# An FNet and GEGLU kernel on one core: width transform ahead of the sequence transform, both by seven products

## The chip, the core and the metric

The kernel runs on one core of one Trainium2 chip, in one launch. TensorE (PE in the profile) multiplies matrices into PSUM, VectorE (DVE) and ScalarE (ACT) do elementwise work, GpSimd (POOL) and SyncE (SP) here issue DMAs. Each engine works through a queue of its own; semaphores tie the queues together. The metric is the device time of a run in microseconds. Before the change the median of three runs is 816.8 us (816.44 to 816.83).

## What is computed

The input x has 2048 rows of 512. Its layer norm xn goes two ways, and both results are added to x:

```python
a = einsum("bsd,ed->bse", x, dft_hid_re)      # x is xn here
b = einsum("bsd,ed->bse", x, dft_hid_im)
y = einsum("ts,bse->bte", dft_seq_re, a) - einsum("ts,bse->bte", dft_seq_im, b)
...
h = gelu(einsum("bsd,df->bsf", x, w_gate)) * einsum("bsd,df->bsf", x, w_up)
return einsum("bsf,fd->bsd", h, w_down)
```

The first three lines are the Fourier branch: a width transform (512 by 512, real and imaginary) and a sequence transform (2048 by 2048, real and imaginary). The last two are the GEGLU branch with 1792 hidden columns. Everything is float32.

## The kernel before

A float32 product is made of three matmuls: each operand is split into a high part (`split_hi`, on ACT, a copy to fp32r, line 68) and a low part (`split_lo`, on DVE, source minus high part, line 73), and `mm3` (line 84) adds high by high, high by low and low by high into one PSUM bank. Every matmul of weight has a 128 by 128 stationary and a 128 by 512 moving operand.

Most products of two matrices cut in 2 by 2 blocks are done with seven block products in place of eight, which needs sums of blocks beforehand on DVE and sums of results afterwards.

The instructions of each engine run in the order in which the program issues them (`tc.manual_schedule()`); what is prepared ahead is written out by hand. The stages in order:

- Normalisation of the 16 panels of x (`ln_begin`, `ln_end`, `ln_split`), mixed with the sequence transform of the first 512 output rows (`seq`, z). That is done plainly: 16 panels, two matrices, four column blocks, three matmuls, 384 in all.
- `y_part` multiplies the result of a chunk of 512 rows by the width matrices (96 matmuls per chunk), `y_store` adds x and stores to HBM (`partial`).
- The three other chunks (`steps`, 24 per two passes): `load_step`, `sum_step` and `split_step` prepare the matrix panels two to four steps ahead, `products` makes 3 or 4 of the seven products of a step, 1008 matmuls in all. Behind each chunk `y_part` follows.
- x is normalised a second time, transposed, in between (`early_xT`).
- 28 units of GEGLU (`unit`), 14 for each half of the rows. A unit makes seven products of 6 matmuls (`product`); `background` lists the work on DVE and ACT that prepares the next units and `run` spreads it over the unit; `fill` puts products of the down projection (`down`, 6 matmuls each) between. Their sums go to `partial` in HBM by accumulating DMAs on POOL.
- `finish` and `last_down` make the output from the seven sums and `partial`.

All SBUF tiles come from one pool of 109 slots of 2 KB per partition. PSUM has 8 banks.

Of the kernel before, what the change touches and what calls it, by code (L numbers as in the profile page):

```python
# [8 lines left out]
F32 = mybir.dt.float32  # L9
# [5 lines left out]
P = 128  # L15
# [8 lines left out]
TPC = CH // P  # L24
SPT = 2 * TPC
HD = D // 2
HS = NS // 2
WARM = 11
SLOTS = 109
# [5 lines left out]
def fnet_geglu_kernel(ctx: ExitStack, tc: tile.TileContext, x, xt, cs, dh, wgu, wd, out):  # L35
# [4 lines left out]

    nc = tc.nc

    const = ctx.enter_context(tc.tile_pool(name="const", bufs=1))
    mem = ctx.enter_context(tc.tile_pool(name="mem", bufs=SLOTS))
# [7 lines left out]

    def ps_tile(name):
        return psum.tile([P, D], F32, name=name, tag="ps")

    def hl_tile(name):

        return slot(name + "h", F32R), slot(name + "l", F32R)  # L60

    def hl_half(name):

        t = slot(name, F32R, (P, 2, HD))
        return t[:, 0], t[:, 1]

    def split_hi(t, src, sign=1):
        nc.scalar.activation(t[0], src, AF.Copy, scale=float(sign))  # L68

    def split_lo(t, src, sign=1, engine=nc.vector):  # L70
        hi = t[0].bitcast(F32)
        if sign > 0:
            engine.tensor_sub(t[1], src, hi)  # L73
        else:
            engine.scalar_tensor_tensor(t[1], src, -1.0, hi, op0=OP.mult, op1=OP.subtract)

    def split(t, src, sign=1, engine=nc.vector):
        split_hi(t, src, sign)
        split_lo(t, src, sign, engine)

    def mm3(ps, a, sl, b, first, last, resumed=False, part=slice(3), late=0):

        for r, (u, v) in list(enumerate(((0, 0), (late, 1 - late), (1 - late, late))))[part]:
            nc.tensor.matmul(ps, a[u][:, sl], b[v], start=first and r == 0, stop=last and r == 2,  # L84
                             skip_group_check=resumed)
# [4 lines left out]
    stats = const.tile([P, 2, NS], F32, name="stats")  # L90
    ident = const.tile([P, P], F32, name="ident")
    eps = const.tile([P, 1], F32, name="eps")
    mean_rstd = dram.tile([2, NS, P], F32, name="mean_rstd")

    partial = dram.tile([NC // 2, 7, 2, P, CH], F32, name="partial")
    xT_hl = dram.tile([7, 2, 2, P, CH], F32, name="xT_hl")
    xnt = dram.tile([NC // 2, 2, ND, P, CH], F32, name="xnt")


    xs, ln, xn = {}, {}, {}  # L100

    def load_x(n):
        if n < NS:
            xs[n] = slot(f"x{n}")
            if n:
                nc.sync.dma_start(xs[n], x[n])
            else:
                for h, queue in enumerate((nc.sync, nc.scalar)):
                    queue.dma_start(xs[n][:, h * HD:(h + 1) * HD], x[n, :, h * HD:(h + 1) * HD])

    def ln_begin(n):
        parts = 1 if n else 2
        bn = small.tile([P, parts, 6], F32, name="bn")
        for h in range(parts):
            nc.vector.bn_stats(bn[:, h], xs[n][:, h * HD:(h + 1) * HD] if parts > 1 else xs[n])
        nc.vector.bn_aggr(stats[:, :, n], bn)
        ln[n] = small.tile([P, 2], F32, name="w")
        nc.scalar.activation(ln[n][:, 0:1], stats[:, 1, n:n + 1], AF.Abs_reciprocal_sqrt, bias=eps)
        nc.scalar.activation(xs[n], xs[n], AF.Identity, bias=stats[:, 0, n:n + 1], scale=-1.0)

    def ln_end(n):
        r, t = (ln[n][:, i:i + 1] for i in range(2))
        var = stats[:, 1, n:n + 1]

        nc.vector.scalar_tensor_tensor(t, var, EPS, r, op0=OP.add, op1=OP.mult)
        nc.vector.scalar_tensor_tensor(t, t, 0.5, r, op0=OP.mult, op1=OP.mult)
        nc.vector.scalar_tensor_tensor(var, t, 1.5, r, op0=OP.subtract, op1=OP.mult)
        xn[n] = hl_half(f"xa{n}"), hl_half(f"xb{n}")
        for h in range(2):
            nc.scalar.activation(xn[n][h][0], xs[n][:, h * HD:(h + 1) * HD], AF.Copy, scale=var)  # L130
        nc.scalar.activation(xs[n], xs[n], AF.Copy, scale=var)

    def ln_split(n):
        ln.pop(n)
        for h in range(2):
            split_lo(xn[n][h], xs[n][:, h * HD:(h + 1) * HD])


    seq = [(n, m) for n in range(NS - 2) for m in range(2)]
    seq += [(n, m) for m in range(2) for n in (NS - 2, NS - 1)]  # L140
    raws, panels, dhl = {}, {}, {}

    def load_panel(i):
        if i < len(seq):
            n, m = seq[i]
            raws[i] = slot("pan")
            nc.sync.dma_start(raws[i], cs[0, m, n])

    def split_panel(i, part=slice(2)):
        if i < len(seq):  # L150
            if part.start is None:
                panels[i] = hl_tile("pan")
                split_hi(panels[i], raws[i])
            if part.stop is None or part.stop == 2:
                split_lo(panels[i], raws.pop(i))

    draw = {}

    def load_d(i):
        if 0 <= i < 2 * ND:  # L160
            draw[i] = slot("d")
            nc.sync.dma_start(draw[i], dh[i // ND, i % ND])

    def split_d(i, part):
        if 0 <= i < 2 * ND:
            if part == 0:
                dhl[divmod(i, ND)] = hl_tile(f"d{i}")
# [46 lines left out]

    yps, yx = {}, {}

    def load_y(c):
        for j in range(TPC):
            yx[j] = slot("yx")
            nc.sync.dma_start(yx[j], xt[c // 2, c % 2, j])  # L220

    Y_ORDER = [(1, 0), (1, 1), (0, 2), (0, 3), (1, 2), (1, 3), (0, 0), (0, 1)]
    Y_FIRST = [(m, d) for m in range(2) for d in range(ND)]

    def y_part(q, js=range(TPC), order=Y_ORDER):

        for j in js:
            if q == 0:
                yps[j] = ps_tile("y")
            for part in (slice(2), slice(2, 3)):  # L230
                for r in range(2):
                    m, d = order[2 * q + r]
                    mm3(yps[j], dhl[m, d], cols(j), z[m, d], q == r == 0, q == 3 and r == 1, part=part, late=1)

    def y_store(c, js=range(ND)):

        sp, t = divmod(c, 2)
        for j in js:
            nc.vector.tensor_add(yx[j], yps[j], yx[j])
        for j in js:  # L240
            if t and j < 2:
                nc.vector.tensor_sub(yx[j], yx[j], yx[j + 2])
            nc.sync.dma_start(partial[sp, (1, 3, 2, 4)[2 * t + j // 2], j % 2], yx[j])

    def store_stats():
        ps = ps_tile("st")
        nc.tensor.transpose(ps[:2 * NS, :P], stats.rearrange("p a b -> p (a b)"), ident)
        t = slot("st")
        nc.vector.tensor_copy(t[:2 * NS, :P], ps[:2 * NS, :P])
        nc.sync.dma_start(mean_rstd.rearrange("a b c -> (a b) c"), t[:2 * NS, :P])  # L250

    PANELS = {0: ((0, 0), (1, 0), (1, 1)), 1: ((0, 0), (1, 0), (0, 1), (1, 1))}
# [726 lines left out]
```

## Time and profile before

| | us |
|---|---|
| median of three runs | 816.8 |
| span of the profiled execution | 815.6 |
| PE busy | 810.1 |
| DVE busy | 703.6 |
| ACT busy | 478.7 |
| POOL busy | 97.1 |

The profile shows one execution. Busy times are the union of an engine's instructions, so two that overlap count once. "Releaser" is the instruction whose end let another start. A timeline row has the start in us from the span's start, the duration in us, engine, line, operation, outputs and inputs, shapes and count. A window row has the width of a stretch, busy times of PE, PEld (weight loads), DVE, ACT and POOL with the number of instructions in brackets, the granted clock, the share of the DMA engines that was busy, and GB/s.

### The profile page before, as it was taken

How to read it: one execution, taken by the hardware profiler on the slowest of the kernel's cores; microseconds unless marked ns; L12 is line 12 of the kernel's file. 1: busy time of each engine (PE TensorE's matmuls, PEld its weight loads, DVE VectorE, ACT ScalarE, POOL GpSimd, SP SyncE). 2: the span in 40 equal slices, each digit the busy share in tenths (PEclk: the TensorE clock that was granted, in tenths of full speed). 3: DMA queues.
4: the chain of work that ended last, by engine and by line, in shares of the span. 5: the costliest groups of instructions: out<-in, count | busy, mean ns of one | idle time of the engine just before them, and what ended most of it. 6: DMA issues, size and time to landing. Idle time of an engine off the chain costs nothing. (4 is left out here: it accounts for less than half of the span.)

```text
span 815.6 us, 11284 instructions
## 1 busy us (share of the span) xinstructions
PE 810.1 (99%) x3558; PEld 665.5 (82%) x3558; DVE 703.6 (86%) x1300; ACT 478.7 (59%) x910; POOL 97.1 (12%) x132
## 2 busy tenths in 40 slices
PE   9999999999999999999999999999999999999998
PEld 6888888888888888888788888888888888888886
DVE  6677998998899997999779998888787778989787
ACT  6787535543255343644366768767666777675564
POOL 0000000000100000000001412422221233222100
PEclk9999999999999999999999999999999999999999
DMA  9900438664796838763332967768976787787942
GB/s 329 378 16 1 168 130 282 196 191 150 245 371 205 276 123 302 257 227 104 119 115 80 259 138 155 171 138 200 262 127 123 129 220 157 165 209 138 246 106 104
DMA packets 79084, 149.15 MB, mean 183 GB/s; under 512 B 9104, under 2 KB 9648, under 8 KB 79024
## 3 DMA queue, kind: packets, MB, share of 16 engines
q1 hardware_dynamic: 63408, 115.13, 42.5%
q0 software_dynamic: 15328, 33.04, 21.9%
q8 instruction: 28, 0.46, 0.2%
q14 instruction: 32, 0.26, 0.1%
q10 hardware_dynamic: 288, 0.26, 0.1%
HBM read 106.95 MB, written 41.44 MB: 182 GB/s over the span
## 5 line engine op out<-in xcount | busy, mean ns | idle before, releaser
L68 ACT ACTIVATE psh<-pan 128x512 fp32r<-128x512 f32 x168 | 97.0, 626 | 107.8 <-DVE pan L281 32.2
L73 DVE TENSOR_TENSOR psl<-pan,psh 128x512 fp32r<-128x512 f32 x168 | 105.5, 685 | 3.7 <-ACT psh L68 3.5
L543 POOL DMA_DIRECT2D partial<-part x82 | 71.9, 894 | 222.6 <-ACT part L539 201.9
L84 PE MATMUL m<-psl,xch 128*128 128x512 f32 x192 | 74.9, 390 | 0.3 <-DVE psl L73 0.3
L84 PE MATMUL m<-psh,xch 128*128 128x512 f32 x192 | 74.8, 390 | 0.0
L84 PE MATMUL m<-psh,xcl 128*128 128x512 f32 x192 | 74.7, 389 | 0.0
L539 ACT ACTIVATE part<-dn 128x512 f32<-128x512 f32 x94 | 55.4, 605 | 24.2 <-PE dn L84 22.4
L73 DVE TENSOR_TENSOR wl<-ws,wh 128x512 fp32r<-128x512 f32 x84 | 55.0, 684 | 0.1
L68 ACT ACTIVATE wh<-ws 128x512 fp32r<-128x512 f32 x84 | 49.4, 629 | 0.0
L766 DVE TENSOR_TENSOR w<-c,w 128x512 f32<-128x512 f32 x28 | 19.3, 690 | 31.8 <-ACT w L763 31.8
L763 ACT ACTIVATE w<-b 128x512 f32<-128x512 f32 x28 | 16.8, 598 | 49.1 <-PE b L84 49.1
L84 PE MATMUL z<-panh,xa 128*128 128x512 f32 x128 | 44.7, 390 | 0.0
L84 PE MATMUL z<-panh,xb 128*128 128x512 f32 x128 | 44.6, 389 | 0.0
L393 POOL DMA_DIRECT2D xnt<-xr x16 | 8.9, 555 | 297.9 <-DVE xr L382 297.9
L84 PEld LDWEIGHTS m<-psl,xch 128*128 128x128 f32 x192 | 36.0, 188 | 8.4 <-DVE psl L73 1.0
L84 PEld LDWEIGHTS m<-psh,xch 128*128 128x128 f32 x192 | 36.0, 188 | 7.6
L84 PEld LDWEIGHTS m<-psh,xcl 128*128 128x128 f32 x192 | 36.0, 188 | 7.4
L73 DVE TENSOR_TENSOR htl<-s,hth 128x512 fp32r<-128x512 f32 x56 | 36.0, 686 | 5.2 <-ACT hth L68 5.2
L512 DVE TENSOR_TENSOR s<-s 128x512 f32<-128x512 f32 x56 | 37.5, 688 | 1.0
L73 DVE TENSOR_TENSOR wl<-wx,wh 128x512 fp32r<-128x512 f32 x28 | 19.2, 687 | 19.3 <-ACT wh L68 19.3
L68 ACT ACTIVATE hth<-s 128x512 fp32r<-128x512 f32 x56 | 32.4, 643 | 2.0 <-DVE s L512 2.0
L84 PE MATMUL m<-psh,xa 128*128 128x512 f32 x96 | 33.5, 389 | 0.0
(393 smaller groups left out, 2357.7 us busy)
## 6 DMA issues: line engine op xcount, KB each, us to landing
pan<-in_cs SPq DMA_DIRECT2D x200, 256.0 KB, 4.4
partial<-part POOLq DMA_DIRECT2D x94, 256.0 KB, 4.7
wx<-in_wgu SPq DMA_DIRECT2D x56, 256.0 KB, 4.6
wd<-in_wd SPq DMA_DIRECT2D x28, 256.0 KB, 4.3
acc<-partial SPq DMA_DIRECT2D x28, 256.0 KB, 5.2
yx<-in_xt SPq DMA_DIRECT2D x16, 256.0 KB, 4.4
partial<-yx SPq DMA_DIRECT2D x16, 256.0 KB, 2.3
xr<-in_xt SPq DMA_DIRECT2D x16, 256.0 KB, 5.1
```

What stands on the lines that cost most here:

```text
L68: nc.scalar.activation(t[0], src, AF.Copy, scale=float(sign))
L73: engine.tensor_sub(t[1], src, hi)
L84: nc.tensor.matmul(ps, a[u][:, sl], b[v], start=first and r == 0, stop=last and r == 2, skip_group_check=resumed)
L393: nc.gpsimd.dma_start(xnt[sp, t, d], xr[sp, d, t])
L512: nc.vector.tensor_sub(t, u, v)
L539: nc.scalar.activation(t, ps[j], AF.Copy)
L543: nc.gpsimd.dma_start(partial[sp, r, j], t, accum_op=OP.add)
L763: nc.scalar.activation(w, b, AF.Copy)
L766: nc.vector.tensor_add(w, c, w)
```

## The change

The width transform comes first. `spectral(sp, k, i)` makes product k of seven for panel i of a half (`sp`) of the rows: 6 matmuls, with the transposed x as stationary and the width matrices (`w1`) as moving operand. The first half's transposed x is made on PE from the normalised panels (`transpose_x`); its seven block operands xT stay for the first 14 units. The results a and b go to HBM (`ab`). The matrices w1 (seven pairs of high and low tiles) and the second half's xT are parked in HBM (`park`, on POOL) and fetched again (`fetch`, on SP) around unit 13; behind unit 13 stands spectral of the second half, then units 14 to 27.

The sequence transform comes last, as 4 passes of 16 steps (`steps`), for both halves of the output. It goes on in PSUM banks that are seeded from the down projection's sums in `partial`: three products per step in the first two passes, four in the last two. Its panels come from HBM as before; a and b are loaded and split beside the first pass (`early_side`) and the second (`late_side`). `drain` makes the output. x itself enters through DMAs from `xt` to `partial` in HBM and through `load_residual`. SBUF is now 43 slots of 4 KB per partition and 23 of 2 KB.

The core of the diff (the old stages named above go; unit keeps its seven products):

```diff
-WARM = 11
-SLOTS = 109
+WARM = 12
+BIG = 43
+SLOTS = 23
...
+    def first_half(n):
+        b11, b21 = halves(pts[n])
+        split_hi(xT_part(0, n), b11)
+        split_hi(xT_part(1, n), b21)
+        xq[n] = slot("xq")
+        nc.scalar.activation(xq[n], pts[n], AF.Copy)
+        split_lo(xT_part(0, n), b11)
+        split_lo(xT_part(1, n), b21)
...
+    def spectral(sp, k, i):
...
+        for j in range(2):
+            mm3(ps[i], [v[:, j] for v in xT[k]], cols(i), [v[:, j] for v in w1[k]], k in (0, 4) and j == 0, j == 1,
+                resumed=k not in (0, 4))
+        if k == 0:
...
+            nc.scalar.activation(sb[i], sa[i], AF.Copy)
...
+        elif k == 6:
+            s6[i] = slot("s6")
+            nc.scalar.activation(s6[i], sb[i], AF.Copy)
+        elif k == 3:
+            t = slot("b")
+            nc.scalar.activation(t, sb[i], AF.Copy, scale=-1.0)
+            to_ab(n, 1, t)
+        elif k == 4:
+            neg_sub(s6[i], sa[i], s6[i])
+            to_ab(n + TPC, 1, s6[i])
...
+    for n in range(TPC, SPT):
+        transpose_x(n)
+        second_half(n)
+        if n + 1 < SPT:
+            ln_apply(n + 1)
+        split(xT_part(5, n - TPC), xsum[n - TPC][5])
+        spectral(0, 5, n - TPC)
...
+    def side_work(k, f, src):
+        for j in range(2):
+            if f:
+                f(j)
+            w1_part(k, src, slice(j, j + 1))
+        for i in range(TPC):
+            split(xT_part(k, i), xsum[i][k])
...
+    side_work(*more[0])
+    for k, (f, *rest) in zip((6, 3, 4), more[1:]):
+        for i in range(TPC):
+            spectral(0, k, i)
+        side_work(f, *rest)
+    add_w(0)
+    split_w(0)
...
         def multiply(k, ps, first=False):
             product(n, k, ps, first)
-            if (n, k) in FETCH:
-                fetch_xT(FETCH[n, k])
+            if n == NP - 1:
+                xT[k] = fetch(xT_hl, k, "xT")
+                if k == 0:
+                    w1[0] = fetch(w1_hl, 0, "w1")
...
+    for p, k in enumerate(S_ORDER):
+        for i in range(TPC):
+            spectral(1, k, i)
+            if i == 0:
+                while carry:
+                    carry.pop(0)()
+                if p + 1 < len(S_ORDER):
+                    w1[S_ORDER[p + 1]] = fetch(w1_hl, S_ORDER[p + 1], "w1")
+    for n in range(NP, 2 * NP):
+        unit(n)
...
+    while carry:
+        carry.pop(0)()
+    for i in range(SUM_AHEAD):
+        sum_step(i)
+    for k in range(4):
+        h_sum(NP - 1, k)
+    for i in range(SPLIT_AHEAD):
+        split_step(i)
+    for n in range(SIDE_AHEAD):
+        early_side(n)
...
+    def contract(i, r, j):
+        c, g, n = steps[i]
+        mm3(bank[c, r, j], side(r, n), cols(j), pan_hl[i, r], False, n == NS - 1, resumed=True)
```

`S_ORDER` is (0, 1, 5, 6, 3, 4, 2). The head before the loop over panels 4 to 7 prepares panels 0 to 3 one by one: `ln_stats`, `ln_first`, `ln_apply`, `transpose_x`, `first_half`, `w1_part`, with `spectral(0, 0, i)` and `spectral(0, 1, i)` between, and then `w1_sums` with `w1_part(5)` and the statistics of panels 4 to 7. `background` of units 0 and 1 takes the statistics of the second half's panels, units 4 and 5 normalise its transposed rows (`norm_xr`), and units 6 to 11 split and park them. The last four `spectral(0, 2, i)` are items between the products of units 0 and 1.

More of the change, by code (lines that the diff above doesn't have):

```diff
@@ L65, in hl_half, with split_hi, split_lo, split @@
         return t[:, 0], t[:, 1]
[L67 to L83, printed above, removed]
+    def split_hi(t, src):
+        nc.scalar.activation(t[0], src, AF.Copy)
+    def split_lo(t, src):
+        nc.vector.tensor_sub(t[1], src, t[0].bitcast(F32))
+    def split(t, src):
+        split_hi(t, src)
+        split_lo(t, src)
+    def neg_sub(dst, u, v):
+        nc.vector.scalar_tensor_tensor(dst, u, -1.0, v, op0=OP.mult, op1=OP.subtract)
+    def mm3(ps, a, sl, b, first, last, resumed=False, late=0):
+        for r, (u, v) in enumerate(((0, 0), (late, 1 - late), (1 - late, late))):
             nc.tensor.matmul(ps, a[u][:, sl], b[v], start=first and r == 0, stop=last and r == 2,
@@ L133, in ln_split @@
[L133 to L155, printed above, removed]
@@ L225, in y_part, with ln_scale @@
[L225 to L243, printed above, removed]
+    def ln_scale(n0, n1, rstd):
+        var = stats[:, 1, n0:n1]
+        w = small.tile([P, 2, n1 - n0], F32, name="w")
+        r, t = w[:, 0], w[:, 1]
+        nc.scalar.activation(r, var, AF.Abs_reciprocal_sqrt, bias=eps)
+        nc.vector.scalar_tensor_tensor(t, var, EPS, r, op0=OP.add, op1=OP.mult)
+        nc.vector.scalar_tensor_tensor(t, t, -0.5, r, op0=OP.mult, op1=OP.mult)
+        nc.vector.scalar_tensor_tensor(rstd, t, 1.5, r, op0=OP.add, op1=OP.mult)
@@ new lines, in w1_part, with transpose_x, halves @@
+    def w1_part(k, src, j=slice(2), part=slice(2)):
+        if k not in w1:
+            w1[k] = [pair(f"w1{k}{h}") for h in "hl"]
+        t = [v[:, j] for v in w1[k]]
+        for f in (split_hi, split_lo)[part]:
+            f(t, src[:, j])
+    def transpose_x(n):
+        pts[n] = ps_tile("pt")
+        for j in range(ND):
+            nc.tensor.transpose(pts[n][:, cols(j)], xs[n][:, cols(j)], ident)
+    def halves(t):
+        v = t.rearrange("p (h j t) -> p h j t", h=2, j=2)
+        return v[:, 0], v[:, 1]
@@ L518, in h_split @@
         return hl[q, r], hs[q, H_PLACE[(1, 3, 0, 2)[k]]]
[L520 to L524 removed]
+    D_ORDER = (0, 2, 1, 5, 4, 6, 3)
     def down(qs, r, js):
@@ L671, in background @@
             for f in weight_sums(("d", n // 2)):
-                work.append((None, f, 1))
+                put(f, cost=1)
         else:
@@ L691, in background @@
-        return work
-    FETCH = {(NP - 3, 2): 0, (NP - 2, 4): 4, (NP - 2, 2): 5, (NP - 1, 5): 1}
-    ends = {}
+                put(f, cost=1)
+        if n < 2:
+            for i in range(4):
+                put(ln_stats, SPT + 4 * n + i)
+        if n == 2:
+            put(ln_scale, SPT, NS, stats[:, 1, SPT:], cost=1)
+            put(store_stats, cost=1)
+        if n in (4, 5):
+            for h in range(2):
+                for j in range(2):
+                    put(norm_xr, h, n - 4, j, cost=4)
@@ new lines, in fnet_geglu_kernel @@
+    for k in range(7):
+        xT[k] = [pair(f"xT{k}{h}") for h in "hl"]
+    ln_stats(0)
+    ln_first(0, 1)
+    ln_apply(0)
+    w1_part(0, wraw[0], slice(0, 1))
+    transpose_x(0)
+    ln_stats(1)
+    ln_first(1, 2)
+    first_half(0)
+    ln_apply(1)
+    w1_part(0, wraw[0], slice(1, 2))
+    spectral(0, 0, 0)
+    transpose_x(1)
+    w1_part(1, wraw[1], slice(0, 1))
+    w1_part(1, wraw[1], slice(1, 2))
+    first_half(1)
+    ln_stats(2)
+    ln_stats(3)
+    ln_first(2, 4)
+    spectral(0, 1, 0)
@@ new lines, in fnet_geglu_kernel, with w1_sums @@
+    spectral(0, 0, 1)
+    ln_apply(2)
+    transpose_x(2)
+    first_half(2)
+    spectral(0, 1, 1)
+    ln_apply(3)
+    spectral(0, 0, 2)
+    transpose_x(3)
+    first_half(3)
+    s1, s2 = pair("s1", F32), pair("s2", F32)
+    a11, a12, a21, a22 = (wraw[b] for b in range(4))
+    def w1_sums(j):
+        nc.vector.tensor_add(s1[:, j], a21[:, j], a22[:, j])
+        nc.vector.tensor_sub(s2[:, j], s1[:, j], a11[:, j])
+    for j in range(2):
+        w1_sums(j)
+        w1_part(5, s2, slice(j, j + 1))
```

831 lines of the change are left out of this document (357 added, 474 removed).

## The prediction

> **What bounds the kernel now.** First the page's head, busy line and slices.
>
> ```profile
> span 815.6 us, 11284 instructions
> PE 810.1 (99%) x3558; PEld 665.5 (82%) x3558; DVE 703.6 (86%) x1300; ACT 478.7 (59%) x910; POOL 97.1 (12%) x132
> PE   9999999999999999999999999999999999999998
> ```
>
> PE is busy in every slice, so a matmul less saves its pitch, and PE idleness costs in full. Next the timeline of PE in a dense stretch (57 matmuls from the first row to the last), and PE's last matmul.
>
> ```profile
> 499.66 0.39 PE L84 MATMUL dn<-hh,wh 128*128 128x512 f32 x1
> ...
> 512.35 0.39 PE L84 MATMUL a<-xT10h,wl 128*128 128x512 f32 x1
> ...
> 811.53 0.28 PE L84 MATMUL dn<-htl,w 128*128 128x256 f32 x1
> ```
>
> The pitch is (512.35 - 499.66) / 56 = 0.2266 us, not the 0.39 of one. From PE's end at 811.8 to the span's end are 3.8 us. Then the timeline of the start:
>
> ```profile
> 1.19 4.58 PE L819 MATMUL warm<-warm 128*128 128x512 bf16 x11 [1.19 <-DVE eps L816]
> 3.23 0.75 DVE L115 BATCH_NORM_STATS2 bn<-x 128x6 f32<-128x256 f32 x2 [2.09 <-DMA x<-in_x]
> 4.02 0.21 DVE L116 BATCH_NORM_AGGREGATE stats<-bn 128x2 f32<-128x12 f32 x1
> 4.27 0.29 ACT L118 ACTIVATE w<-stats,eps 128x1 f32<-128x1 f32 x1 [1.81 <-DVE stats L116]
> 4.47 0.70 ACT L119 ACTIVATE x<-x,stats 128x512 f32<-128x512 f32 x1
> 4.60 0.16 DVE L125 SCALAR_TENSOR_TENSOR w<-stats,w 128x1 f32<-128x1 f32 x1
> 4.98 0.16 DVE L127 SCALAR_TENSOR_TENSOR stats<-w 128x1 f32<-128x1 f32 x1
> 5.79 0.69 DVE L115 BATCH_NORM_STATS2 bn<-x 128x6 f32<-128x512 f32 x1
> 5.80 0.50 PE L84 MATMUL z<-panh,xa 128*128 128x512 f32 x1
> 6.52 0.18 DVE L116 BATCH_NORM_AGGREGATE stats<-bn 128x2 f32<-128x6 f32 x1
> ```
>
> The first real matmul starts at 5.80. A result reaches the next engine about 0.05 us after its end (4.23 to 4.27, 4.56 to 4.60). Now starts of neighbours on DVE and ACT, since instructions overlap there as well:
>
> ```profile
> 485.94 2.74 DVE L512 TENSOR_TENSOR s<-s 128x512 f32<-128x512 f32 x4
> 495.81 0.42 DVE L448 TENSOR_TENSOR ws<-wx 128x256 f32<-128x256 f32 x1
> 496.26 0.43 DVE L448 TENSOR_TENSOR ws<-ws,wx 128x256 f32<-128x256 f32 x1
> 496.61 0.42 DVE L448 TENSOR_TENSOR ws<-wx 128x256 f32<-128x256 f32 x1
> 497.28 0.68 DVE L73 TENSOR_TENSOR xT20l<-xr,xT20h 128x512 fp32r<-128x512 f32 x1
> 497.88 0.68 DVE L73 TENSOR_TENSOR xT21l<-xr,xT21h 128x512 fp32r<-128x512 f32 x1
> ...
> 484.03 0.62 ACT L68 ACTIVATE wh<-wx 128x512 fp32r<-128x512 f32 x1
> 484.55 0.62 ACT L68 ACTIVATE wh<-ws 128x512 fp32r<-128x512 f32 x1
> 488.11 0.59 ACT L494 ACTIVATE s<-a 128x512 f32<-128x512 f32 x1
> 488.59 0.60 ACT L539 ACTIVATE part<-dn 128x512 f32<-128x512 f32 x1
> 489.59 0.43 ACT L68 ACTIVATE w<-wx 128x256 fp32r<-128x256 f32 x1
> 489.89 1.68 ACT L68 ACTIVATE hth<-s 128x512 fp32r<-128x512 f32 x3
> ```
>
> DVE's pitch is 0.60 for 512 wide, 0.35 for 256, 0.45 where it reads its predecessor's result, and a chain of four takes 2.7. ACT's is 0.52 (0.48 out of PSUM), 0.30 for 256 wide; latencies 0.62 and 0.43. Last, three stages (width, then PE, PEld, DVE, ACT, POOL busy, clock, DMA share, GB/s), POOL's costliest group, and the one transpose:
>
> ```profile
> 20.00:30.00 10.00, 10.00 (x46) 8.28 (x45) 6.81 (x20) 7.38 (x16) 0.00 (x0) 1.00 1.05 386
> 140.00:180.00 40.00, 40.00 (x179) 33.10 (x178) 39.42 (x64) 21.86 (x40) 0.00 (x0) 1.00 0.65 192
> 500.00:540.00 40.00, 40.00 (x178) 33.12 (x177) 35.42 (x68) 28.09 (x55) 12.35 (x17) 1.00 0.78 183
> L543 POOL DMA_DIRECT2D partial<-part x82 | 71.9, 894 | 222.6 <-ACT part L539 201.9 <-ACT w L68 12.3 <-ACT s L494 3.4
> L247 PE MATMUL st<-ident,stats x1: 271/271/271, 114.8 to 114.8; 128*32 128x128 f32 x1
> ```
>
> DVE can be 98% busy (39.42 of 40) with PE full, and DMA gives 386 GB/s at most. The old order is prepared steps ahead; that is what keeps PE fed.
>
> **What the change does to PE.** Removed: 384 matmuls of z, 4 x 96 of y, 1008 of the three chunks' steps, together 1776. Added: spectral 2 x 7 x 4 x 2 x 3 = 336, contract 2 x 7 x 16 x 2 x 3 = 1344 in four passes of 16 steps, together 1680. GEGLU (1176) and down (588) stay. So 3444 for 3540, or -96 x 0.2266 = **-21.8 us**. Of 32 transposes of x (0.27 us or less each), the time is in the chain below.
>
> **The head.** The program sets each engine's order, as the rows above show (rsqrt, apply, then the next panel), so an instruction that waits holds all behind it. I follow the queues. Panel 0 is normalised at 6.1 (statistics, rsqrt, four small DVE operations, 0.70), transposed at 6.75. ACT's next is panel 1's rsqrt, which waits for DVE (low part of w1, then 0.69 + 0.18, to 8.2), so it splits panel 0 only then; copy 9.6, normalise panel 1 10.2, w1 high 10.7, DVE low 11.4, first product done 12.1 instead of running since 5.8. Then on ACT: copy 12.75, w1 block 1 13.8, split panel 1 14.9; DVE's low parts 15.25, statistics of 2 and 3 to 16.8; ACT rsqrt, two copies, panel 2 normalised 18.7, transposed 19.35. The same links for panel 3 end at 25.5. w1_sums and w1_part(5) go DVE, ACT, DVE twice, 2 x 2.6, to 29.2; ACT's copies of PSUM queue behind them (29.4); four ln_stats of 0.78 to 32.3; scale and normalise 34.1. PE is idle 25.5 to 29.45 and 30.8 to 34.1.
>
> Panels 4 to 7: transposes 0.6, copy 0.65, four 256-wide DVE sums and a low split 1.95, four matmuls 0.9. PE takes the next transposes only behind spectral(0, 5), so these add up: 4.15 x 4, to 51.
>
> Products 6, 3, 4: side_work for the next follows spectral in the program, so ACT first waits to copy the fourth PSUM bank; behind that copy are the w1 and xT high splits, behind those DVE's low parts, and for all of them PE waits. Per product 4 x 1.36 of matmuls and 2.6 exposed (copy 0.6, two highs 1.1, xT high and low 0.85), 8.0. The first ends at 60.4 (the sum a21 is before it), then 68.4 and 76.4. Product 2 is put off, but its side_work (neg_sub, two sums, two high-low round trips 4.0, four lows 1.4), add_w(0) 1.5 and the first low split 0.7 stand before unit 0's first low part: **unit 0 from 84**, with 144 matmuls done. Bounds: DVE alone (statistics and scales 9.2, w1 lows 14 x 0.60, xT lows 28 x 0.35, w1 sums 5, panel sums 6, drains 2.4, weights 2.2, in all 43, from 3.2) gives 46. The xT splits write strided and partly read PSUM, which no row shows; as fast as the contiguous 256-wide row is what I take, twice as slow adds 10 and gives 94, and a gain stays inside the lower bound.
>
> **The middle.** Spectral(1, 1) needs w1 block 1, in SP's order behind seven xT pairs, w1 block 0 and the weights: 10.4 MB, at 386 GB/s 27 us. From unit 13's start there are 60 x 0.2266 = 13.6 plus 24 x 0.2266 = 5.4, 19 in all, so 8 us are late, and none if free tiles let SP start that much sooner. SP holds load_wd behind these; POOL's queue gains 32 stores of a and b and 28 parks at 0.9 each; POOL has the time (12.35 of 40), and only tiles to be freed wait for it, but its bytes share the DMA engines. I take 6, within 0 to 14. The Trainium skill, Perfetto Trace Analysis, Roofline, puts the ceiling of the 16 DMA engines at about 435 GB/s; by it 10.4 MB take 24 us, and 5 would be late. The rows here stop at 386.
>
> **Units.** Ordinary DVE work per unit is about 11 us beside 12 to 15 of PE. norm_xr adds 8 x 0.65 to units 4 and 5, where fewer fills leave PE 12.2 and 10.9: DVE lags by 8.6, most of which the next banks and units take up. Taken 2 (0 to 8). ln_stats, the negated multiply and the parks are under the same PE cover; without it they would cost their 0.6 each.
>
> **Into the contraction.** Behind unit 27's last matmul DVE has, in order: q6, a half split, three carry operations (3.0), two sum_steps 1.2, four h_sums 2.7, three low panels 1.8, early_side 1.9. PE has nothing to do for 10 us. Iteration 0 adds four h_split lows, so step 1 waits about 3 more. Taken **13** (8 to 16).
>
> **Contraction.** First pass: DVE 0.60 + 3 x 0.60 + 1.6 + 0.35 + 0.60 and a wait of 0.35 are 5.3, PE 24 x 0.2266 = 5.44 while fills last, 4.08 after. The second: DVE 3.6, PE 4.08; then 4.3 and 5.44. All under the 98% seen; panels ask 188 to 257 GB/s. Taken 3 for joints (0 to 12), and 2 for scattered gaps, as the old stream lost 811.8 - 5.8 - 3540 x 0.2266 = 3.8.
>
> **Clock after idleness.** The 11 warm-up matmuls show a PE out of idleness: 0.43 apart (4.58 with one latency), against 0.2266 later. 4.6 us so cost 2.2. Two gaps far over 4 us (10 and 5.5) give 4; none gives 0, six gaps 13. The Trainium skill, TensorE: Matmul & The Clock Gate, Part 1, says that an idle window of about 3.4 us halves the clock until about 3.4 us of work; by it four such gaps cost 4 x 1.7 = 7. The granted-clock column reads 1.00 throughout, so the trace cannot confirm it.
>
> **Sum.** 84 + (3444 - 144) x 0.2266 (747.8) + 6 + 2 + 13 + 3 + 2 + 4 + 3.8 = 865.6 against the execution's 815.6. The median stands 1.2 above that execution, so **867**. Time saved on PE is 21.8; idleness added is about 72: head 84 - 5.8 - 144 x 0.2266 = 45.6, then 6, 2, 13, 3 and 4, and 2 in place of 3.8.
>
> **Rivals.** (1) *Head overlaps*: if queues run past the waits I put into products 6, 3, 4 and panels 4 to 7, DVE's work alone sets the head, 46 for 84: 829. For it: DVE's 43 of 81 us is little over half; against: strict order in the rows. 10%. (2) *Not slower*: the one mechanism is PE cover: PE's own work bounds the new order as it did the old. Then 3444 x 0.2266 + 5.8 + 3.8 + 4 of gaps is 794, 795 as median. It decides once added idleness is below 21.8 us, which asks that 50 of the 72 go, the head's 38 over DVE's work and the 13 for example. For it: the old kernel's 99%; against: each wait stands in the written order. 11%. Between it and (1), about even: 2%. (3) *Memory pools*: 43 large and 23 small slots are nearly full; SP's loads and POOL's slow stores hold slots, and the middle takes 14, the joints 12, units 8: +23, 890. 12%. (4) The products not falling to 3444 is excluded by the count.
>
> **How the numbers follow.** Forecast 65%. With (2) and the even case left out (13%), the range must reach down to (1) and up to (3), whose own spreads add a few: 826 to 891. It holds each term at either of its bounds with the rest as taken. A measurement tells 0.2%. Faster 0.11, same 0.02, slower 0.87.
>
> **What would show it.** PE's slices below 6 until about 84 us; ACT w1 highs waiting for PE banks; a PE hole near 10 us ahead of contract; a hole behind spectral(1, 0) that ends with w1's fetch. A head ending before 60, or no hole ahead of contract, breaks the forecast.

## The result and the profile after

| | before | after | forecast |
|---|---|---|---|
| median, four runs each | 816.6 us (816.4 to 816.8) | 942.1 us (939.6 to 945.3) | 867 (826 to 891) |
| span of the profiled execution | 815.6 | 943.5 | 865.6 |

The ratio is 1.154 (95% interval 1.152 to 1.156): slower, as forecast, but by 125 us and not by 50; the time lies outside the range. The head of the page of after, busy times, and the slices of PE and of its granted clock:

```profile
span 943.5 us, 11396 instructions
PE 835.5 (89%) x3490; PEld 669.8 (71%) x3490; DVE 694.2 (74%) x1282; ACT 514.4 (55%) x971; POOL 144.1 (15%) x206
PE   7566796877999939999999997699988999999998
PEclk7768798899999969999999999799998999999999
```

3490 matmuls are the 3444 of the count, 12 warm-up ones and 34 transposes, so the products fell as counted. PE lost its density: 15 of the 40 slices are below 9, where one was. The clock row, all nines before, dips in ten of these fifteen slices. DVE has less to do than before (694.2 for 703.6) and is no bound over the whole.

The stages can be read from one instruction. In a unit, ACT copies the first product's bank (L505, `b<-a`) when that product is done. Timeline of ACT, units 0, 13, 14 and 27 (start, duration, idle time before):

```profile
100.33 0.58 ACT L505 ACTIVATE b<-a 128x512 f32<-128x512 f32 x1 [1.79 <-PE a L82]
...
311.87 0.58 ACT L505 ACTIVATE b<-a 128x512 f32<-128x512 f32 x1 [0.34 <-PE a L82]
...
384.54 0.58 ACT L505 ACTIVATE b<-a 128x512 f32<-128x512 f32 x1 [10.90 <-PE a L82]
...
570.89 0.63 ACT L505 ACTIVATE b<-a 128x512 f32<-128x512 f32 x1
```

The matmuls between two marks times the pitch of 0.2266 give what a PE without a wait would take. Units 0 to 4 issue 54 matmuls each, unit 5 48, later ones 66 (even) or 60; unit 13 to 14 issues 60 and 168 of spectral.

| stage | measured | PE alone | idle | forecast idle |
|---|---|---|---|---|
| head, to unit 0's first product | 100.3 | | | 85.4 by the forecast, so 14.9 over |
| units 0 to 12 | 211.5 | 172.7 | 38.8 | 2 |
| unit 13 and spectral(1) | 72.7 | 51.7 | 21.0 | 6 |
| units 14 to 26 | 186.3 | 186.3 | 0 | 0 |

The rest shows in stretches of 20 us, where a full PE has 90 matmuls: from 580 to 620 there are 83 too few, 18.8 us; between passes 0 and 1 of the contraction 44, 10.0 us. Windows, columns as before:

```profile
580.00:600.00 20.00, 7.08 (x26) 5.43 (x25) 15.21 (x28) 9.96 (x20) 1.75 (x2) 0.66 0.88 292
600.00:620.00 20.00, 17.52 (x71) 14.06 (x70) 17.76 (x35) 10.96 (x23) 2.48 (x3) 0.91 0.86 250
...
680.00:700.00 20.00, 18.82 (x81) 14.59 (x80) 17.37 (x31) 17.18 (x34) 5.88 (x8) 1.00 1.08 321
700.00:720.00 20.00, 14.55 (x55) 11.54 (x54) 13.24 (x23) 10.04 (x18) 1.61 (x3) 0.83 1.03 352
...
760.00:780.00 20.00, 18.38 (x78) 14.03 (x77) 17.18 (x28) 15.65 (x29) 7.54 (x10) 1.00 1.06 271
840.00:860.00 20.00, 19.57 (x86) 15.51 (x85) 16.36 (x26) 13.92 (x26) 0.00 (x0) 1.00 0.62 214
860.00:880.00 20.00, 19.65 (x87) 15.96 (x86) 18.33 (x30) 9.28 (x17) 0.00 (x0) 1.00 1.01 368
```

The later joints lack 12, 4 and 3: 4.3 us. Against the terms of the sum the excess is 14.9 (head) + 36.8 (units) + 15.0 (middle) + 5.8 (into the contraction, 18.8 for 13) + 9.3 (joints and scattered gaps, 14.3 for 5), less the 4 booked for the clock, which these stages already contain: 77.8, and 865.6 + 77.8 = 943.4.

### The profile page after: what moved, and what is told of

It reads as the page before. It is cut to its first block, busy times and chain, and to the rows that moved or that the text cites. A ratio compares the mean times of both kernels' runs of the same rounds, so it can differ in the third digit from the quotient of the medians.

```text
span 943.5 us, 11396 instructions
## 1 busy us (share of the span) xinstructions
PE 835.5 (89%) x3490; PEld 669.8 (71%) x3490; DVE 694.2 (74%) x1282; ACT 514.4 (55%) x971; POOL 144.1 (15%) x206
## 4 chain that ended last, share of the span: by engine, by line
PE 56%; issue 13%; DMA 12%; DVE 10%; ACT 5%; POOL 3%; SPq 0%; POOLq 0%; DVEq 0%; ACTq 0%
PE m L82 27%; PE dn L82 7%; PE b L82 6%; PE sb L82 4%; PE sa L82 4%; PE a L82 4%; DMA pan<-in_cs 4%; PE c L82 4%; POOL partial L391 3%; DMA partial<-part 2%; DMA xT6l<-xT_hl 1%; DMA w10l<-w_hl 1%; DMA acc<-partial 1%; DMA ab<-s 1%; DMA w11l<-w_hl 1%
## 5 line engine op out<-in xcount | busy, mean ns | idle before, releaser
L68 ACT ACTIVATE ps<-pan 128x512 fp32r<-128x512 f32 x224 | 128.0, 624 | 93.9 <-DVE pan L565 41.7
L71 DVE TENSOR_TENSOR ps<-pan,ps 128x512 fp32r<-128x512 f32 x224 | 141.2, 685 | 12.4 <-ACT ps L68 12.1
L82 PE MATMUL m<-ps,s 128*128 128x512 f32 x384 | 94.4, 395 | 0.1
L82 PE MATMUL m<-ps,qr 128*128 128x512 f32 x384 | 93.4, 391 | 1.2 <-DVE ps L71 0.9
L82 PE MATMUL m<-ps,bt 128*128 128x512 f32 x384 | 92.6, 390 | 1.2 <-ACT m L628 1.2
L82 PEld LDWEIGHTS m<-ps,s 128*128 128x128 f32 x384 | 73.8, 192 | 16.3 <-ACT m L628 0.6
L82 PEld LDWEIGHTS m<-ps,qr 128*128 128x128 f32 x384 | 71.7, 188 | 17.9 <-DVE ps L71 2.1
L82 PEld LDWEIGHTS m<-ps,bt 128*128 128x128 f32 x384 | 71.8, 188 | 17.0 <-ACT m L628 2.2
L82 PE MATMUL dn<-h,wh 128*128 128x512 f32 x252 | 64.5, 390 | 3.3 <-DVE h L71 3.3
L82 PE MATMUL dn<-ht,wh 128*128 128x512 f32 x252 | 63.9, 389 | 0.0
L82 PEld LDWEIGHTS m<-ps,a 128*128 128x128 f32 x192 | 37.5, 198 | 31.7 <-ACT m L628 13.3
L82 PE MATMUL a<-xT0h,wh 128*128 128x512 f32 x112 | 42.0, 416 | 10.4 <-ACT wh L68 9.2
L520 DVE TENSOR_TENSOR w<-c,w 128x512 f32<-128x512 f32 x28 | 19.3, 691 | 42.4 <-ACT w L517 42.3
```

Of the source, the lines that this page charges most:

```text
L68: nc.scalar.activation(t[0], src, AF.Copy)
L71: nc.vector.tensor_sub(t[1], src, t[0].bitcast(F32))
L520: nc.vector.tensor_add(w, c, w)
```

## What each hole waits for

**Head.** Windows, and two matmuls of spectral(0, 5) of one panel, the first and the last of six:

```profile
20.00:40.00 20.00, 10.69 (x42) 7.33 (x42) 10.36 (x26) 10.25 (x20) 2.89 (x6) 0.89 0.37 118
40.00:60.00 20.00, 13.42 (x36) 9.21 (x36) 6.86 (x19) 6.51 (x13) 2.61 (x6) 0.59 0.32 106
60.00:80.00 20.00, 14.49 (x48) 10.85 (x48) 5.96 (x13) 9.27 (x20) 1.33 (x3) 0.75 0.04 17
```
```profile
40.18 0.80 PE L82 MATMUL sb<-w15h,xT5h 128*128 128x512 f32 x1 [2.06 <-ACT xT5h L68]
...
42.48 0.63 PE L82 MATMUL sb<-w15h,xT5l 128*128 128x512 f32 x1
```

Six matmuls take 42.48 + 0.63 - 40.18 = 2.93 us; the forecast had 0.9 for four. Between 40 and 60 the granted clock is 0.59, with DVE and ACT a third busy and DMA at 0.32: a chain of waits, and each link that runs on PE runs at half rate. A single wait can be enough. After 17 matmuls at full rate (66.44 to 70.13 us, 0.23 apart) PE waits 2.09 us; two matmuls later they are 0.43 apart, and the granted clock from 73.4 to 76.2 us is 0.50:

```profile
70.13 0.39 PE L82 MATMUL sb<-w16h,xT6l 128*128 128x512 f32 x1
72.60 0.50 PE L82 MATMUL sb<-w13h,xT3h 128*128 128x512 f32 x1 [2.09 <-ACT xT3h L68]
...
74.04 0.63 PE L82 MATMUL sb<-w13h,xT3h 128*128 128x512 f32 x1
74.46 0.63 PE L82 MATMUL sb<-w13l,xT3h 128*128 128x512 f32 x1
```

**Units.** PE's four largest waits from 100 to 240 us (total, times, longest), and three instructions behind them on ACT and DVE:

```profile
PE st L246 <- DVE stats L136: 6.8, 1, 6.8
PE b L82 <- ACT w L517: 6.7, 2, 5.9
PE b L82 <- ACT b L505: 4.7, 1, 4.7
PE a L82 <- ACT wh L68: 3.5, 1, 3.5
```
```profile
115.25 0.63 ACT L347 ACTIVATE s<-w 128x512 f32<-128x512 f32 x1 [3.81 <-DMA ab<-s]
...
152.06 0.17 DVE L136 SCALAR_TENSOR_TENSOR stats<-w 128x8 f32<-128x8 f32 x1
...
223.27 0.63 ACT L68 ACTIVATE xU6h<-xr 128x512 fp32r<-128x512 f32 x1 [5.67 <-DVE xr L272]
```

Four waits, of three kinds. In unit 2 the second of the two transposes of `store_stats` stands in PE's queue and waits for the scaling of the statistics (L136): ACT's part of it ends at 148.6, but on DVE the scaling stands behind weight sums until 151.7. In unit 0 ACT waits for a small slot that a store by POOL still holds (the tile `s` of the first row waits for the DMA `ab<-s`, which takes 9.2 us where its median is 2.4); its weights come late. In unit 3 ACT stands 5.03 us for which the profile names no releaser; that slots are behind it is shown by e_mem27 below. At unit 7's start ACT stands at the split of a sum (xU6) that DVE makes only then, and the first product's copy queued behind that split holds PE; the time falls into unit 6's 23.2 us.

The four waits add up to 21.7 of the 38.8. Windows over the units and over the middle:

```profile
100.33:311.87 211.54, 183.99 (x765) 147.64 (x765) 173.27 (x329) 126.92 (x242) 42.29 (x61) 0.94 0.65 180
311.87:384.54 72.67, 55.57 (x229) 44.38 (x228) 20.51 (x40) 21.21 (x39) 11.97 (x20) 0.88 0.82 295
```

In the units PE stands still for 27.5 us and is busy 184.0 where its matmuls at full clock take 172.7: most of the other 11.3 are matmuls that run below full clock behind the waits (granted 0.94 over the stage). In the middle the same difference is 55.6 - 51.7 = 3.9.

**Middle.** Timeline of SP's issues and of PE around the wait:

```profile
312.14 0.37 SPq L107 DMA_DIRECT2D xT0h<-xT_hl  x1
...
337.73 0.33 SPq L107 DMA_DIRECT2D w11h<-w_hl  x1
```
```profile
331.36 0.39 PE L82 MATMUL sa<-w10h,xT0l 128*128 128x512 f32 x1
346.89 0.77 PE L82 MATMUL sa<-w11h,xT1h 128*128 128x512 f32 x1 [15.15 <-DMA w11h<-w_hl]
```
```profile
312.14:346.89 34.75, 18.09 (x77) 13.94 (x76) 14.07 (x29) 11.36 (x22) 3.31 (x4) 0.84 1.02 354
332.00:352.00 20.00, 4.67 (x10) 3.42 (x11) 0.00 (x0) 0.96 (x2) 0.41 (x1) 0.60 1.03 411
```

The late block is the one that the forecast named, and the DMA engines are full (1.03, 411 GB/s). The block is issued 25.6 us after the first fetch, and PE has it 9.2 us behind that, since what was issued before it is still in flight. From the first fetch to its use are 34.75 us, in which the engines moved 354 GB/s, 12.3 MB.

**Into the contraction and its first joint.** Timelines of ACT, PE and SP:

```profile
594.81 0.63 ACT L68 ACTIVATE s<-s 128x512 fp32r<-128x512 f32 x1 [6.64 <-DVE s L78]
595.34 3.17 ACT L628 ACTIVATE m<-acc 128x512 f32<-128x512 f32 x6
```
```profile
595.98 2.93 PE L82 MATMUL m<-ps,a 128*128 128x512 f32 x6 [12.92 <-ACT m L628]
```
```profile
663.21 9.25 SPq L634 DMA_DIRECT2D xres<-in_xt  x4
```

PE waits 12.92 for the seeds (`m<-acc`), which stand on ACT behind a split that waits for DVE, and again runs six matmuls in 2.93. At the joint SP stands 9.25 at `load_residual`, and the panels queue behind it.

## The experiments

Theory: the head loses by strict order and by a PE at half rate; the units by four separate waits; the middle by bytes; the contraction by DVE's work and by SP's queue. The rivals stand with each run. Each time is of one run unless said otherwise, so it stands against 942.1 (939.6 to 945.3) and says little under 6 us; the stages say more. Head, units 0 to 12, middle (marks 13 to 14) and rest (from mark 27) in us, from the same ACT rows:

| run | time | head | units | middle | rest |
|---|---|---|---|---|---|
| after | 942.1 | 100.3 | 211.5 | 72.7 | 372.6 |
| e_head | 926.4 | 79.5 | 218.0 | 70.2 | 370.6 |
| e_warm | 930.5 | 91.1 | 210.2 | 70.8 | 370.3 |
| e_headwarm | 928.3 | 82.8 | 216.2 | 70.9 | 370.3 |
| e_mem27 | 937.9 | 102.2 | 205.0 | 69.3 | 373.2 |
| e_stats | 937.4 | 100.2 | 204.1 | 73.3 | 371.7 |
| e_nonorm | 940.8 | 100.3 | 207.9 | 72.9 | 371.6 |
| e_spread | 935.6 | 100.4 | 205.8 | 72.8 | 368.4 |
| e_half | 929.6 | 100.1 | 211.1 | 59.6 | 370.7 |
| e_mid | 939.8 | 101.3 | 211.9 | 71.0 | 367.5 |
| e_seed | 939.3 | 101.0 | 211.4 | 70.3 | 368.6 |
| e_queue | 946.8 | 101.0 | 211.4 | 72.7 | 373.4 |
| e_joint | 942.1 | 100.5 | 211.4 | 70.6 | 371.5 |
| e_all | 903.1 | 81.2 | 194.6 | 69.9 | 369.3 |
| e_all3 | 893.0 | 82.6 | 181.4 | 70.2 | 370.7 |
| e_all2 (4 runs) | 889.1 | 82.8 | 180.0 | 70.7 | 368.9 |

Stages that an edit doesn't touch show the noise: head 100.1 to 101.3, units 211.1 to 211.9, middle 70.2 to 73.3, rest 367.5 to 372.6. Most of the spread of whole times is in the last two.

### The head: e_head, e_warm, e_headwarm

e_head puts the next product's preparation ahead of the product, and the next panel's transposes ahead of spectral(0, 5):

```diff
+    transpose_x(TPC)
     for n in range(TPC, SPT):
-        transpose_x(n)
...
             ln_apply(n + 1)
+            transpose_x(n + 1)
         split(xT_part(5, n - TPC), xsum[n - TPC][5])
+    for n in range(TPC, SPT):
         spectral(0, 5, n - TPC)
...
+        side_work(f, *rest)
         for i in range(TPC):
             spectral(0, k, i)
-        side_work(f, *rest)
```

> The head alone is reordered: each side_work is issued ahead of the product that it used to follow, the transposes of panels 4 to 7 ahead of all spectral(0, 5). All sums are the same. If the written order of the queues is what holds the head (a drain on ACT that waits for PE, with the next high splits behind it), the first product of unit 0, which ends at 99.9 us in the changed kernel, ends at 70 to 80, and the kernel at 912 to 922 us. If PE's own slow rate is what holds it, the order matters little: 937 to 945.

The head takes 79.5, 20.8 less, at the upper end of what queue order gives. The units then take 6.5 of it back (218.0), unit 0 most of that (24.4 for 18.6), so the 926.4 lies above the 912 to 922 expected.

e_warm leaves the order and puts 8 to 12 bf16 matmuls without use into PE's waits:

```diff
+            nc.tensor.matmul(ps, warm[:, :P], warm, start=True, stop=True)
...
         transpose_x(n)
+        keep_warm(8)
         second_half(n)
...
+        if k != 4:
+            keep_warm(10)
         side_work(f, *rest)
```

> The head keeps its order; 8 to 12 bf16 matmuls on a tile of zeros fill PE's waits behind each of the transposes of panels 4 to 7 and behind products 5, 6 and 3. If PE runs at half rate because it idled (six matmuls of spectral(0, 5) take 2.93 us, 1.36 elsewhere), these six take 1.4 to 1.5 and the head ends 8 to 14 us sooner: 928 to 935 us. If the slow matmuls have another cause (their operands arriving late), they stay at 2.9 and the time is the same or up to 5 us longer.

The same two matmuls in its timeline:

```profile
40.17 0.50 PE L82 MATMUL sb<-w15h,xT5h 128*128 128x512 f32 x1 [0.33 <-ACT xT5h L68]
...
41.53 0.39 PE L82 MATMUL sb<-w15h,xT5l 128*128 128x512 f32 x1
```

Six matmuls in 41.53 + 0.39 - 40.17 = 1.75 for 2.93, from the same start. The loop over panels 4 to 7, 5.8 us per panel in after, takes 4.3; the forecast had 4.15. The head is 9.2 shorter. Nothing but PE's activity changed, so the half rate is a cause. Of the 14.9 us over forecast at least 9.2 are the clock, and at most 91.1 - 85.4 = 5.7 the chain itself.

> Both head edits at once: the order of e_head and dummy matmuls (nothing but heat, result unused) in PE's waits. Alone they brought the end of unit 0's first product forward by 20.8 us (e_head) and 9.2 (e_warm). If strict order and the half rate after idleness are two separate costs they add: that product ends near 70 and the time is near 915 (942 - 15.7 - 11.6). If both edits recover the same waits (half rate only exists where PE waits): product near 78, time 922 to 926.

Head 82.8, 3.3 longer than with the order alone: the two don't add, and neither expectation held. e_head still has a granted clock of 0.56 from 40 to 50 us, which the dummies raise to 0.81; but 55 dummies take PE's time too. Which of the two decides, no run separates. Where e_head's gain went is seen in the waits of PE from 82 to 130 us:

```profile
PE a L82 <- ACT wh L68: 9.1, 1, 9.1
```

The earlier unit 0 meets the small slots that were late in after too (3.5 there).

### The units: e_mem27, e_stats, e_nonorm, e_spread

e_mem27 has four small slots more and two large ones less:

```diff
-BIG = 43
-SLOTS = 23
+BIG = 41
+SLOTS = 27
```

> 41 slots of 4 KB and 27 of 2 KB in place of 43 and 23, nothing else. If units 0 to 8 lose their 39 us because loads and copies wait for one of the 23 small slots, these units take 15 to 30 us less (139.5 us from the first product of unit 0 to that of unit 8), and the kernel 912 to 930 us, less what two large slots fewer cost later. If DVE's own load in these units is the cause, the units stay within 4 us of 139.5. If the large slots are what is short, the kernel is slower than 942.

Units 0 and 3 (from first product to the next unit's) fall from 18.6 to 14.4 and from 19.8 to 13.3, unit 7 rises from 13.3 to 19.3 with two large tiles less. Slots did cost units 0 and 3; the whole stage gains 6.5. From unit 0's first product to unit 8's it takes 134.6 for 139.5, so 4.8 less and not 15 to 30, and 937.9 lies above 912 to 930: slots are one cause of several. The first joint of the contraction gained as well, 17 matmuls short from 660 to 720 (86, 85 and 82 in the three windows) where after has 44:

```profile
680.00:700.00 20.00, 19.32 (x85) 15.33 (x84) 16.72 (x28) 17.54 (x34) 7.49 (x10) 1.00 1.09 319
...
700.00:720.00 20.00, 18.40 (x82) 14.91 (x81) 17.69 (x30) 13.02 (x24) 0.00 (x0) 1.00 1.04 389
```

The rest as a whole is no shorter, though, 373.2: the later joints lack more (70 and 74 matmuls from 740 to 760 and 840 to 860), and the wait ahead of the contraction was longer in that run.

e_stats moves `store_stats` to the start of unit 3, and all that follows from it by one unit.

```diff
-            put(store_stats, cost=1)
...
         if n == 3:
+            store_stats()
+        if n == 4:
             for t in range(2):
                 load_st(t)
```

> store_stats, which puts two transposes into PE's queue at the end of unit 2 where they wait 6.8 us for DVE, moves to the start of unit 3, and what follows from it (norm_xr, sums_xr, t4_xr, the splits and parks) one unit later. If that wait is time lost by itself: 5 to 8 us less, 934 to 938 us. If DVE or the slots set the pace of units 0 to 8 anyway, the wait turns up elsewhere and the time is within 3 us of 942.

Units gain 7.4, but not in unit 2, which keeps 22.6: the start of unit 3's code still lies ahead of unit 3's first product, and the second transpose waited 6.7, as before. The edit missed its aim; unit 3 (12.5) and the later shift gained, so that 937.4 lies in the first range expected is luck.

e_nonorm normalises only one of four blocks of the second half's transposed input (12 of 16 operations on DVE left out).

> Of the 16 DVE operations that normalise the transposed x of the second half in units 4 and 5, 12 are left out (one block of four keeps its normalisation), loads and all else stay. Units 4 to 7 take 64.7 us from first product to first product where their matmuls take 51.7. If DVE's load is what is late there, 12 x 0.65 = 7.8 us of it go and 7 to 11 us of the 13 with them: 931 to 936. If slots or DMAs hold these units, they lose less than 3: 939 to 945.

Units 4 to 6 fall by 5.5 in all (12.2, 13.8 and 19.8 us for 12.2, 15.9 and 23.2), the stage by 3.6. That is between the two expectations. With three quarters of that work gone unit 6 still takes 4.9 more than PE alone: DVE's load is a part, ACT's wait for the sum another. e_spread leaves the work and moves it (two pieces in each of units 4 to 7, sums in unit 8, no split right behind its sum):

> The normalisation of the second half's transposed input is spread over units 4 to 7 (two pieces each in place of four in units 4 and 5), its sums go to unit 8, and no split of a sum stands right behind the sum. DVE theory (DVE full at 180 to 220 us holds ACT and PE): units 4 to 6 fall to at most 12.5, 12.5 and 16 us, unit 7's first product waits no more, 5 to 9 us gone: 933 to 937. Rival (small slots and DMA latency hold units 3 to 7 whatever DVE does): units 3 to 8 keep their sum within 2 us, 940 to 944.

```diff
-        if n in (4, 5):
+        if n in (4, 5, 6, 7):
...
-        if n == 6:
+        if n == 8:
...
-        for k in {6: (6,), 7: (0, 1), 8: (5,), 9: (2,), 10: (4,), 11: (3,)}.get(n, ()):
+        for k in {6: (0,), 7: (1,), 8: (2,), 9: (6,), 10: (5,), 11: (4,), 12: (3,)}.get(n, ()):
```

Units 4 to 6 take 12.3, 12.4 and 15.2, within 1.9 us of what PE alone needs; 11.4 us are gone there, 5.7 in the stage, since units 7 and 9 give 8.0 back. So not the amount of DVE work cost that time but its place.

### The middle: e_half, e_mid

e_half fetches half of each tile, so the products of the second half use half of the data twice:

```diff
-            nc.sync.dma_start(t[h].bitcast(F32).rearrange("p a b -> p (a b)"), src[k, h])
-        return t
+            nc.sync.dma_start(t[h][:, 0].bitcast(F32), src[k, h, :, :CH])
+        return [v[:, 0:1].broadcast_to([P, 2, D]) for v in t]
```

> Every fetch around unit 13 brings half of each parked tile, and the same half is used twice, so the products of the second half of the rows are not the reference's. Same instructions on PE, ACT and DVE, same order, same tiles, half of 14.7 MB. From the first product of unit 13 to that of unit 14 the changed kernel takes 72.7 us where 228 matmuls are 51.7. If bytes on the DMA engines make that hole, it falls from 21 to 3 to 8 us and the kernel to 924 to 931. If tiles that are not free hold SP back, or the order of its queue, the hole stays above 14.

The middle falls to 59.6, by 13.1, to 8.0 over PE alone. One wait of 5.5 is left. e_mid keeps the bytes and fetches the late block three pairs sooner, and each later block one product sooner:

```diff
-                if k == 0:
-                    w1[0] = fetch(w1_hl, 0, "w1")
+                if k in (0, 1):
+                    w1[k] = fetch(w1_hl, k, "w1")
...
-                if p + 1 < len(S_ORDER):
-                    w1[S_ORDER[p + 1]] = fetch(w1_hl, S_ORDER[p + 1], "w1")
+                if p + 2 < len(S_ORDER):
+                    w1[S_ORDER[p + 2]] = fetch(w1_hl, S_ORDER[p + 2], "w1")
```

> Only the order of fetches in the middle: block 1 of the first weights is fetched behind xT1 in unit 13, ahead of the pairs xT6, xT3 and xT2, and each later block one product sooner. Bytes are the same. If the wait of 15.1 us is an order (the block that is needed second stands behind seven pairs and the down weights), the stretch from unit 13's to unit 14's first product falls from 70 to 73 us to 56 to 62 and the time to 928 to 934. If it is bytes or full tiles, the wait only comes later, at another block or pair: 68 to 73 us, 939 to 945.

The largest waits of PE in the middle of e_mid:

```profile
PE sa L82 <- DMA w11h<-w_hl: 6.1, 1, 6.1
PE sb L82 <- DMA w15h<-w_hl: 4.0, 1, 4.0
PE sb L82 <- DMA w15l<-w_hl: 1.4, 1, 1.4
```

The one wait of 15.1 has become three of 11.5 in all, and the stage is 71.0, within its noise. Bytes, not their order, make most of this hole.

### The contraction: e_seed, e_queue, e_joint

e_seed issues the seeds and step 0's panels and side work ahead of what is left of unit 27.

> At the step from unit 27 to the contraction the program order is changed: the six seeds of PSUM banks first, then panels and side of step 0, then the rest of unit 27 (carry, h_sum). In the changed kernel PE stands from 583.7 to about 596.6 us, 12 to 13 us, and works at half rate after. If queue order on ACT and DVE is what holds it, the hole falls to 5 to 7 us and the kernel to 933 to 938 us. If the late landing of the first panels (SP issues twelve loads from 571 to 585) holds it, the hole stays above 10 us and the time is within 3 us of 942.

PE starts again at 585.4 instead of 596.0, after 4.2 us, but then waits in steps 0 and 1 (PE's waits from 560 to 612):

```profile
PE m L82 <- ACT a L68: 5.5, 2, 4.2
PE m L82 <- DVE a L71: 4.4, 2, 2.6
PE m L82 <- DVE ps L71: 0.3, 1, 0.3
```

The rest is 368.6, within the noise: part of the hole moved behind step 0, and the matmuls there run below full clock (0.82 and 0.84 from 580 to 620). DVE is busy 18.5 of the 20 us from 580 to 600, so the sum of its work, which the edit only reorders, is the likely bound; no run takes any of that work away, so this is not shown.

e_queue moves the loads of the residual, the ends and the sums from SP's queue to POOL's; e_joint leaves the queue and issues the first two three steps and the sums two steps sooner.

```diff
-                nc.sync.dma_start(late[c, h, j], xt[c, 1, 2 * h + j])
+                nc.gpsimd.dma_start(late[c, h, j], xt[c, 1, 2 * h + j])
... (the same for the ends and the sums)
```
```diff
-        if n == NS - 3:
+        if n == NS - 6:
...
-        if n == NS - 2 and p + 1 < len(passes):
+        if n == NS - 4 and p + 1 < len(passes):
```

> The loads of the residual, of the ends and of the seeds' sums go through POOL's queue in place of SP's, so that panel loads do not stand behind them there. In the changed kernel SP stands 9.25 us at load_residual (663 to 672) and PE then loses 9 us at 700 to 710, 2.6 near 770 and 1.5 near 860. If SP's order is the cause, these holes go and the kernel takes 929 to 935 us. If the DMA engines are simply full there (321 to 352 GB/s), the holes stay: 939 to 945.

> In the contraction the residual's and the ends' loads are issued three steps sooner and the next pass's sums two steps sooner; nothing else. If the hole of about 10 us between passes 0 and 1 comes from bytes that all want to move in the last three steps, it shrinks to 2 to 5 us: 935 to 939. If it comes from slots that are full (a load that waits holds SP's queue, the panels behind it are late), the wait only moves forward and grows: 941 to 947.

Neither closes the hole. From 660 to 720 after has 226 matmuls (90, 81 and 55; e_mid, which leaves this stage alone, has 232), e_queue 211 and e_joint 223 (86, 64 and 73). e_queue takes 946.8, above both of its ranges. In e_joint the hole moves forward and the time is 942.1, as expected for full slots. So the 9.25 us of SP at `load_residual` were where it showed and not why; with more small slots (e_mem27) 253 came, which speaks for slots too. What part of it is the DMA engines (321 to 352 GB/s at a share over 1) stays open.

### All together: e_all, e_all3, e_all2

e_all is e_headwarm with e_stats and e_mem27.

> e_headwarm with e_stats (statistics stored one unit later) and e_mem27 (27 small slots, 41 large tiles). If the four causes are separate, single gains add to 15.7 + 11.6 + 4.7 + 4.2 = 36: 906. If slots, statistics and cold PE all fill the same idle time in units 0 to 3, the last two add nothing: 915 or what e_headwarm gives. In no case as low as 880: the hole in the middle (21), the one ahead of the contraction (18) and that between its passes (10) are untouched.

39.0 gained, 36.0 of it in the head and the units. e_headwarm, e_stats and e_mem27 alone gained 13.8 + 4.7 + 4.2 = 22.7. Its first mark of unit 0 is at 81.18, that of unit 1 at:

```profile
93.49 0.58 ACT L506 ACTIVATE b<-a 128x512 f32<-128x512 f32 x1 [0.16 <-PE a L82]
```

So unit 0 takes 12.3 us, where e_headwarm took 22.9: the slots had swallowed what the head gained. Units 2 and 7 kept 22.6 and 21.5. e_all3 puts the statistics' transposes into the middle of unit 3's work (`put(store_stats, cost=1)` there), spreads the normalisation as in e_spread one unit later, and takes e_mid's fetches; e_all2 adds the dummies.

> e_head, e_mem27 and e_mid, with the statistics of the second half stored in the middle of unit 3's work and its normalisation spread as in e_spread; without dummy matmuls. If unit 2's 22.6 us and unit 7's 21.5 us in e_all were PE's queue behind the statistics' transposes and ACT behind a split of a sum, both fall to 12 to 16 us: 15 us less than e_all, less e_mid's gain, 876 to 890 with e_mid's theory of order, 884 to 895 without. If slots or DMA hold these units, both keep 20 us: 890 to 903.

> The same with the dummy matmuls of e_headwarm in PE's waits. If the half rate still costs once the order is mended: 5 to 12 us under e_all3. If the dummies only take places that PE would have used, as e_headwarm against e_head (928.3 for 926.4) leaves possible: within 3 us of e_all3. Either way it stays over the 816 of before, since the idleness ahead of the contraction and the head's chain remain.

e_all3: units 2 and 7 fall to 16.0 and 13.7, the stage to 181.4; 893.0 lies in the range without a gain from e_mid's order. e_all2: 889.1 (887.4 to 890.6; ratio to before 1.088, interval 1.086 to 1.090), 4 under e_all3, of which 1.2 lie ahead of unit 13 and the rest in the noise, so the dummies add little to a mended order. All waits of 1 us and more that PE has left between 80 and 260 us:

```profile
PE dn L82 <- DVE h L71: 2.2, 2, 1.3
PE b L82 <- ACT w L517: 1.2, 1, 1.2
PE a L82 <- DVE wh L71: 1.1, 1, 1.1
```

The units now lose 180.0 - 172.7 = 7.3. No version came under the 816 of before: the head (82.8), the middle's bytes and the way into the contraction remain.

## Why the prediction was wrong

- **PE's count** held: 3444 products, -21.8 us.
- **Units, 2 us (0 to 8): the step that failed most.** It measured 38.8. The prediction compared DVE's amount of work with PE's time per unit and booked only where the sum exceeded it ("most of which the next banks and units take up"). The runs show four waits, 21.7 us, that no such sum contains: PE's queue behind the statistics' transposes and ACT's behind a split of a sum (mended by order alone: e_spread and e_all3), and, in units 0 and 3, small slots (e_mem27). Behind the waits the matmuls run below full clock, most of another 11.3. With slots, order and places mended the units lose 7.3 (e_all2). The rule that an instruction that waits holds all behind it was used for the head, where it was right, and not for the units. Rival (3) named the pools and gave the units 8 for them; slots gave 6.5 alone and hid some 10 more, unit 0's 22.9 against 12.3.
- **The middle, 6 us (0 to 14)**: right mechanism, named with its block (w1 block 1), but 21.0. PE's cover of 19 us was right (19.6). The size that failed is the 27 us from the first fetch to the block: they were 34.75, for 12.3 MB at 354 GB/s and not 10.4 MB at 386. Beside the 15.1 of that wait stand 1.9 of smaller ones and 3.9 of matmuls below full clock. The Trainium skill, Perfetto Trace Analysis, Roofline, has about 435 GB/s as the ceiling; the 411 of the window here lie nearer to that than the 386 at which the forecast's rows stopped.
- **The head, 84**: the order was right, and e_head, by changing that order alone, took 20.8 us off. Its chain was up to 5.7 short, and the clock cost at least 9.2 in it.
- **Clock, 4 us (0 to 13)**: the mechanism was right; only gaps far over 4 us had been counted. It cost at least 9.2 in the head (e_warm), and, inside the terms above, most of 11.3 in the units and of 3.9 in the middle. In after the granted clock shows it, as it did not before. The Trainium skill, TensorE: Matmul & The Clock Gate, Part 1, halves the clock after an idle window of about 3.4 us; by it the forecast's four gaps gave 7. The rows of after agree on the half rate (0.43 us from start to start for 0.23), but not on the wait: one of 2.09 us was enough.
- **Into the contraction, 13 (8 to 16)**: mechanism right, measured 18.8, part of it six matmuls at half rate. **Joints, 3 (0 to 12) and 2**: 14.3, most of it at the first joint.
- **Rivals.** The head did not overlap, and PE's cover did not return. The signs that the forecast named mostly came (the hole ahead of the contraction, the one behind spectral(1, 0) that ends with w1's fetch), but they say nothing of size. Range: five terms (head, units, middle, the way in, the joints) came out above their upper bounds together. The range let one term at a time go to its bound, while slots, DMA and cold PE pushed several the same way.

## What to carry to other kernels

A schedule written by hand has to be followed queue by queue through every stage, not only through the start: an average of DVE or ACT work under PE's time says nothing of one instruction that stands first in a queue and waits. A wait of PE costs twice where its matmuls run at half rate behind it. When an edit frees time, look at the next stage before booking it: here one gain reached the end only after the slots behind it had been widened. And a transfer that is needed at a given time costs its turn behind all bytes already in flight, beside its own.

## What the runs showed of the hardware

- One wait of 2.09 us, behind 17 matmuls at full rate, was followed by matmuls 0.43 us apart at a granted clock of 0.50. With waits of about 2 us between groups of six matmuls PE stayed near half rate: 2.93 us for 1.75 with dummies in the waits, granted clock 0.59 over 20 us for 1.00.
- The DMA engines gave 411 GB/s over 20 us, more than the 389 that before shows from 10 to 20 us. A transfer of 512 KB could then be used 9.2 us after its issue.
